# The second tile's first products taken beside the first tile's, with the same weight parts, while the weights are still being converted

## The chip, the cores and the metric

The kernel runs on one core of one Trainium2 chip. Its metric is device time in microseconds; the time of a version is the median of several executions. A profiled execution is recorded separately, with every instruction of the engines: TensorE (PE, its weight loads PEld), VectorE (DVE), ScalarE (ACT), GpSimd (POOL) and SyncE (SP, which issues the DMAs). Every engine takes its instructions in the order in which the program lists them, so an instruction that waits holds up all that stand behind it on its engine.

## The reference

Attention with pooled keys and values, then a gated feed-forward block on its output:

```python
# q, k, v: (8, 8, 576, 64) = batch, heads, sequence, head size; pool = 8, so 72 pooled keys
k_p = k.reshape(B, H, Sp, pool, D).mean(axis=3)
v_p = v.reshape(B, H, Sp, pool, D).mean(axis=3)
scores = scale * np.matmul(q, k_p.transpose(0, 1, 3, 2))
scores = scores - np.max(scores, axis=-1, keepdims=True)
attn = np.exp(scores)
attn = attn / (np.sum(attn, axis=-1, keepdims=True) + 1e-09)
x = np.matmul(attn, v_p)            # then heads are joined: 4608 tokens x 512
a = x @ w_a                         # 512 x 1536
b = x @ w_b                         # 512 x 1536
return (a * b @ w_out)              # 1536 x 512
```

The queries, keys and values are float32; the weights reach the chip as 64-bit floating-point words, which the kernel converts to float32 itself.

## The kernel before

**Precision.** Each float32 operand of a product is split into a high part in the rounded type `fp32r` and a low part, the remainder; a product is then three matmuls (high times high, high times low, low times high). A split is a copy on ScalarE for the high part and a subtraction (`low_part`, L169) on DVE or POOL for the low.

**Tiling.** The 4608 tokens are nine tiles of 512 (`NTILE`). Attention works in 40 chunks of up to 128 tokens that follow the batches (576 tokens each): the first tile has chunks 0 to 3, the second chunks 4 to 8 (of 64, 64, 128, 128 and 128 tokens). A chunk (`chunk`, L343) loads its queries, splits them (`qh`, `ql`), multiplies them with the pooled keys (scores, L379), takes the maximum of each head on DVE (L388, L389), an exponential on ScalarE for each head with its sum (L392), reciprocals (L399, L400) and the normalization (L402, on POOL or DVE), splits the probabilities (`pr`, `rem`), turns them with transposes on TensorE (L447, copied out by ScalarE at L448) and, a block of chunks at a time, multiplies them with the pooled values (L480 to L483). The result is split into `xh` and `xl` (L491 and `low_part`).

**Feed-forward.** For each tile, twelve steps f = 0 to 11 of 128 hidden columns. `ffn_in` (L511) makes 12 matmuls into `psa` and 12 into `psb` (L522 to L524), one PSUM buffer each; ScalarE copies `psa` to `h` (L527, one buffer) and `gated` (L497) multiplies it with `psb` on DVE (L500) and splits the product into `hh` and `hl`. `ffn_out` (L532) of the step before adds 12 matmuls to four accumulators (L543 to L545), which are copied out and stored after the last step (L549 to L552). A step is 36 matmuls; a tile 432.

**Weights.** `convert_weights` (L194) turns the 64-bit words of `w_a`, `w_b` and `w_out` into float32, step by step, with two operations on ScalarE (L210, L211) and three on DVE (L212, L216, L221) for each weight and step; it runs through the first tile, at most two steps ahead. `split_weight` (L228) then makes the parts `jha`/`jla`, `jhb`/`jlb`, `jho`/`jlo`, two buffers each, anew for every tile and step; the low parts of `w_a` and `w_b` are made on DVE in the first tile and on POOL later, those of `w_out` on POOL.

**Order.** The program is listed by hand with a small planner, `Chains` (L71). Each piece of work is a generator that yields after a part of it, with the number of ticks until its next part, or `PE` when it next wants a place on TensorE. `ffn_in` and `ffn_out` call `chains.step()` before every six matmuls: a tick. All pieces due are then listed on their engines, and one that wants TensorE is given its place there. `need` (L507) takes ticks without feed-forward work until something is ready. Ahead of the first product, the program takes ticks until the first tile's attention has been listed (L576). The chunks of the second tile are spread over the steps of the first, 10 ticks apart (`CHUNK_GAP`); those of a later tile are spread over the tile ahead of it. Keys and values of a batch are loaded and pooled by `load_keys` (L238) and `load_values` (L279).

The tag `att` (scores, transposes and value products) has two PSUM buffers, `acc` four. `tmp` is a ring of six buffers for raw queries, conversion intermediates, pooled keys and outputs.

Of the kernel before, what the change touches and what calls it, by code (L numbers as in the profile page):

```python
# [20 lines left out]
P = 128  # L21
# [34 lines left out]

AHEAD = 2
# [4 lines left out]
SPLIT_A, SPLIT_B, SPLIT_O = 1, 4, 4  # L62
PROBS_GAP, VALUE_GAP = 2, 4
CHUNK, CHUNK_LATER, CHUNK_GAP = 34, 32, 10
# [3 lines left out]
EARLY_GAP, VALUES_START, KEYS_START, WEIGHTS_START, CONVERT_AFTER = 1, 2, 4, 10, 5  # L68
# [44 lines left out]
def attn_moe_kernel(ctx: ExitStack, tc: tile.TileContext, q, k, v, vr, wa, wb, wo, out):  # L113
# [3 lines left out]
    ps = ctx.enter_context(tc.tile_pool(name="ps", bufs=1, space=bass.MemoryType.PSUM))  # L117
    chains = Chains()
# [48 lines left out]
    vrems, parts, xtiles, turned, begun = {}, {}, {}, {}, []  # L167
# [26 lines left out]
    def convert_weights(name, j, first):  # L194
# [9 lines left out]
        for f in range(NF):  # L204
# [4 lines left out]
            low, mag = tmp(f"wlow_{name}{f}", I32), tmp(f"wmag_{name}{f}")  # L209
            nc.scalar.activation(mag, hi.bitcast(F32), AF.Abs, scale=SHRINK)  # L210
            nc.scalar.activation(low, lo.bitcast(U32), AF.Copy, scale=2.0**-29)  # L211
            nc.vector.tensor_scalar(  # L212
                out=wi, in0=mag.bitcast(I32), scalar1=0x0FFFFFFF, scalar2=3, op0=ALU.bitwise_and, op1=ALU.logical_shift_left
# [13 lines left out]

    def split_weight(name, x):  # L228
        f = x % NF
        yield from wait(("weight", name, f))  # L230
        hi = sb.tile([P, 512], F32R, tag=f"jh{name}", name=f"jh{name}_{x}")
        lo = sb.tile([P, 512], F32R, tag=f"jl{name}", name=f"jl{name}_{x}")
        nc.scalar.copy(hi, raw[name][:, f, :])  # L233
# [109 lines left out]
    def chunk(i):  # L343
        b, o, n = flat[i]
        t, col = divmod(b * S + o, NT)
        first = i < early
        if first:
            qraw = early_q[:, i]
        else:
            qraw = tmp(f"qraw_{i}").rearrange("p (g s) -> p g s", g=NK)  # L350
            load_raw_queries(i, qraw)
            yield 5
# [6 lines left out]
        yield 1 if first else PROBS_GAP  # L359
# [9 lines left out]
        for g0 in range(0, NK, 2):  # L369
            yield from wait(("keys", b, g0))  # L370
            yield PE
            if first:
                pt = ps.tile([P, 512], F32, tag="acc", name=f"psc_{i}_{g0}", bufs=4)
            else:
                pt = ps.tile([P, 512], F32, tag="att", name=f"psc_{i}_{g0}", bufs=2)
            for j in range(2):
                g = g0 + j
                for x, (qq, w) in enumerate(((qh, 0), (qh, 1), (ql, 0))):
                    nc.tensor.matmul(  # L379
                        pt[:n, j * hk:(j + 1) * hk],  # L380
                        qq[:, g, :n],
                        kd[:, g, w].rearrange("p e s -> p (e s)"),
                        start=(x == 0),
                        stop=(x == 2),
                    )
            hs = slice(2 * g0, 2 * g0 + 4)
            scores = pt[:n, :2 * hk].rearrange("p (h s) -> p h s", h=4)
            nc.vector.tensor_reduce(out=m[:n, hs], in_=scores, axis=AX.X, op=ALU.max)  # L388
            nc.vector.tensor_scalar_mul(m[:n, hs], m[:n, hs], -SCALE)  # L389
            for j in range(4):  # L390
                h = 2 * g0 + j
                nc.scalar.activation(  # L392
                    s[:n, h], scores[:, j], AF.Exp, bias=m[:n, h:h + 1], scale=SCALE, accum_out=z[:n, h:h + 1]
                )
        mark("scores", i)


        yield 1
        nc.vector.tensor_scalar_add(z[:n], z[:n], 1e-9)  # L399
# [18 lines left out]
        yield PROBS_GAP  # L418
# [41 lines left out]
        yield 1 if first else VALUE_GAP  # L460
# [36 lines left out]
    def gated(x, pt, h):  # L497
        hh = sb.tile([P, NT], F32R, tag="hh", name=f"hh_{x}")
        hl = sb.tile([P, NT], F32R, tag="hl", name=f"hl_{x}")
        nc.vector.tensor_tensor(out=h, in0=pt, in1=h, op=ALU.mult)  # L500
        parts["h", x] = hh, hl
        yield 1
# [3 lines left out]

    def need(ready):  # L507
# [148 lines left out]
```

## Time and profile before

| | |
|---|---|
| median of 3 runs | 1119.18 us (1118.94 to 1120.06) |
| the profiled execution, its own time | 1116.74 us |
| its span, from the first to the last instruction | 1115.0 us |
| mean granted TensorE clock | 0.986 |
| TensorE busy, of the span | 1045.9 us (94%) |
| DVE, ACT, POOL busy | 543.8, 594.8, 538.6 us |
| first feed-forward matmul | 59.9 us |
| end of the first tile's output products | 219.3 us |

How to read it: the shares are means over stages that differ. Lines of the timeline give the start, the duration, the engine, the line of the kernel, the operation, output <- input and a count; brackets hold the idle time ahead of it on its engine and what ended it. Matmuls overlap, so the time that one takes from TensorE is the distance between starts, not its duration. A group line gives shapes, count, busy time and mean duration in ns, then the idle time ahead of its instructions. A wait line gives who waited for whom: us in total, times, longest. In a table by stage, each engine's busy time is followed by its number of instructions; PEclk is the granted clock.

### The profile page before, as it was taken

Reading aid. Unit: us, or ns where it says so; the run is one execution under the profiler, and the core shown is the slowest. Engines: PE = TensorE matmul, PEld = TensorE weight load, DVE = VectorE, ACT = ScalarE, POOL = GpSimd, SP = SyncE. Lnnn points to the kernel's source line nnn. Section 1 sums busy time; section 2 is a strip of 40 time slices with the busy share of each in tenths; the row PEclk is TensorE's granted clock in tenths of the full one; section 3 lists DMA queues with packets and bytes.
Section 4 is the critical chain, followed back from the end, with each engine's and each line's share of the span. In section 5 each row is a group of like instructions: output and inputs, shape, how many; then the busy total and the mean of one; then the engine's idle time right before and its main releaser. Section 6 shows DMA issues by size and latency. Waiting matters only on the chain.

```text
span 1115.0 us, 14406 instructions
## 1 busy us (share of the span) xinstructions
PE 1045.9 (94%) x5088; PEld 870.9 (78%) x5088; DVE 543.8 (49%) x839; ACT 594.8 (53%) x1651; POOL 538.6 (48%) x441
## 2 busy tenths in 40 slices
PE   4387888999998999999999999999999999999998
PEld 4276666888887888888887888888887888888887
DVE  7688888632455225632456335643356333332111
ACT  5756766545555455554556455554555455453332
POOL 7102322555555555555556455545546555554442
PEclk9989889999999999999999999999999999999999
DMA  6454443210112001300030003200211020001001
GB/s 209 131 160 123 124 150 126 73 42 1 55 42 85 1 1 41 130 1 1 22 115 14 1 2 102 68 1 1 69 55 48 1 66 1 2 1 38 1 1 38
DMA packets 29879, 59.64 MB, mean 53 GB/s; under 512 B 7120, under 2 KB 7120, under 8 KB 29808
## 3 DMA queue, kind: packets, MB, share of 16 engines
q1 hardware_dynamic: 29808, 58.73, 16.5%
q8 instruction: 40, 0.66, 0.3%
q14 instruction: 31, 0.25, 0.1%
HBM read 49.28 MB, written 9.44 MB: 53 GB/s over the span
## 4 chain that ended last, share of the span: by engine, by line
PE 78%; DVE 13%; ACT 6%; issue 2%; DMA 1%; SPq 0%; DVEq 0%; ACTq 0%
PE psb L522 8%; PE psa L522 8%; PE psa L524 8%; PE psa L523 8%; PE acc L543 8%; PE acc L544 8%; PE acc L545 8%; PE psb L524 8%; PE psb L523 7%; PE psc L379 3%; ACT s L392 3%; DVE vdiag L328 2%; PE ptr L447 2%; DVE vrem L170 1%; DVE h L500 1%
## 5 line engine op out<-in xcount | busy, mean ns | idle before, releaser
L500 DVE TENSOR_TENSOR h<-psb,h 128x512 f32<-128x512 f32 x108 | 74.5, 690 | 310.7 <-PE psb L524 310.6
L170 POOL TENSOR_TENSOR jlb<-wb_raw,jhb 128x512 fp32r<-128x512 f32 x96 | 125.1, 1303 | 201.2 <-ACT jhb L233 201.2
L170 POOL TENSOR_TENSOR jlo<-wo_raw,jho 128x512 fp32r<-128x512 f32 x108 | 152.7, 1414 | 81.0 <-ACT jho L233 51.8
L522 PE MATMUL psb<-xh,jhb 128*128 128x512 f32 x432 | 177.8, 412 | 1.3 <-DVE h L500 1.3
L524 PE MATMUL psb<-xh,jlb 128*128 128x512 f32 x432 | 171.5, 397 | 1.8 <-DVE jlb L170 1.8
L522 PE MATMUL psa<-xh,jha 128*128 128x512 f32 x432 | 172.3, 399 | 0.0
L543 PE MATMUL acc<-jho,hh 128*128 128x512 f32 x432 | 171.5, 397 | 0.0
L527 ACT COPY h<-psa 128x512 f32<-128x512 f32 x108 | 63.5, 588 | 201.9 <-PE psa L524 188.4
L523 PE MATMUL psb<-xl,jhb 128*128 128x512 f32 x432 | 170.8, 395 | 0.0
L524 PE MATMUL psa<-xh,jla 128*128 128x512 f32 x432 | 170.1, 394 | 0.0
L523 PE MATMUL psa<-xl,jha 128*128 128x512 f32 x432 | 169.6, 393 | 0.0
L544 PE MATMUL acc<-jlo,hh 128*128 128x512 f32 x432 | 169.5, 392 | 0.0
L545 PE MATMUL acc<-jho,hl 128*128 128x512 f32 x432 | 169.2, 392 | 0.0
L392 ACT ACTIVATE s<-psc,m 128x72 f32<-128x72 f32 (+1 forms) x320 | 97.9, 318 | 133.1 <-DVE m L389 131.7
L170 POOL TENSOR_TENSOR jla<-wa_raw,jha 128x512 fp32r<-128x512 f32 x96 | 138.4, 1442 | 44.1 <-ACT jha L233 43.7
L402 POOL TENSOR_TENSOR s<-s,z 128x576 f32<-128x576 f32 (+1 forms) x38 | 46.1, 1213 | 223.7 <-PE psb L524 141.0
L170 DVE TENSOR_TENSOR hl<-h,hh 128x512 fp32r<-128x512 f32 x108 | 125.8, 1165 | 38.2 <-ACT hh L503 38.0
L503 ACT CAST hh<-h 128x512 fp32r<-128x512 f32 x108 | 67.1, 622 | 89.4 <-DVE h L500 89.2
L524 PEld LDWEIGHTS psb<-xh,jlb 128*128 128x128 f32 x432 | 82.4, 191 | 20.8 <-DVE jlb L170 2.7
L524 PEld LDWEIGHTS psa<-xh,jla 128*128 128x128 f32 x432 | 81.9, 190 | 17.5
L545 PEld LDWEIGHTS acc<-jho,hl 128*128 128x128 f32 x432 | 81.8, 189 | 17.4
L543 PEld LDWEIGHTS acc<-jho,hh 128*128 128x128 f32 x432 | 81.9, 190 | 16.2
(84 smaller groups left out, 1806.3 us busy)
## 6 DMA issues: line engine op xcount, KB each, us to landing
out<-y SPq DMA_DIRECT2D x36, 256.0 KB, 2.1
kraw<-in_k SPq DMA_DIRECT2D x28, 288.0 KB, 3.4
vraw<-in_v SPq DMA_DIRECT2D x28, 256.0 KB, 3.3
qraw<-in_q SPq DMA_DIRECT2D x28, 256.0 KB, 3.7
words<-in_wa SPq DMA_DIRECT2D x12, 512.0 KB, 3.7
words<-in_wb SPq DMA_DIRECT2D x12, 512.0 KB, 3.6
words<-in_wo SPq DMA_DIRECT2D x12, 512.0 KB, 3.6
vraw<-in_vr SPq DMA_DIRECT2D x14, 192.0 KB, 2.7
```

What stands on the lines that cost most here:

```text
L170: eng.tensor_tensor(out=lo, in0=src, in1=hi.bitcast(F32), op=ALU.subtract)
L392: nc.scalar.activation(s[:n, h], scores[:, j], AF.Exp, bias=m[:n, h:h + 1], scale=SCALE, accum_out=z[:n, h:h + 1])
L402: (nc.vector if first and i % 2 else nc.gpsimd).tensor_tensor(out=s[:n], in0=s[:n], in1=z[:n].unsqueeze(2).broadcast_to([n, H, SP]), op=AL ...
L500: nc.vector.tensor_tensor(out=h, in0=pt, in1=h, op=ALU.mult)
L503: nc.scalar.copy(hh, h)
L522: nc.tensor.matmul(pt, wh[:, c], xh[:, kk], start=(kk == 0), stop=False)
L523: nc.tensor.matmul(pt, wh[:, c], xl[:, kk], start=False, stop=False)
L524: nc.tensor.matmul(pt, wl[:, c], xh[:, kk], start=False, stop=(kk == NK - 1))
L527: nc.scalar.copy(h, pt)
L543: nc.tensor.matmul(acc[c], hh[:, cs], wh, start=(f == 0), stop=False)
L544: nc.tensor.matmul(acc[c], hh[:, cs], wl, start=False, stop=False)
L545: nc.tensor.matmul(acc[c], hl[:, cs], wh, start=False, stop=(f == NF - 1))
```

## The change

The steps of feed-forward work become an explicit list, `order`. In the first tile, from step f = 4 (`LAG`) on, `ffn_in` of the first tile is followed by `ffn_in` of the second for the same f, which uses the same parts of `w_a` and `w_b`; then comes `ffn_out` of the first tile for f - 1. The second tile's gated products of these eight steps are not split at once: they are stored to DRAM (`later`) and fetched back (`fetch_gated`) when the second tile's output products want them. After the first tile, the second does its steps f = 0 to 3 and all of its output products. Tiles from the third on run as before.

For this all chunks of the second tile have to be finished before its step 4; they start from tick 14 of the opening on, 3 ticks apart, with shorter gaps between their parts. The loads of the second batch's keys start 4 ticks later. Starts of weight splits, fetches and chunks are now planned from each item's place in `order`.

Three smaller edits go with it. The softmax subtracts the maximum on DVE, takes one exponential over all heads of a chunk on ScalarE and sums on DVE. From chunk 9 (`SUMMED`) on, the two score matmuls with the same high part of the queries become one of 288 columns, whose halves DVE adds. The magnitude in `convert_weights` is written into the weight's own tile rather than into a temporary.

The places of the parts are counted: `room` lets a split begin only in the order of use and while fewer than two parts of its kind are held, and `drop` gives them back after their last use.

```diff
+SUMMED = 9
+LAG = 4
+IN, OUT = 4, 2
+LEAD_A, LEAD_B, LEAD_O, LEAD_H = 5, 4, 6, 8
 PROBS_GAP, VALUE_GAP = 2, 4
-CHUNK, CHUNK_LATER, CHUNK_GAP = 34, 32, 10
+CHUNK = 32
+SECOND_GAP, SECOND_START = 3, 14
-EARLY_GAP, VALUES_START, KEYS_START, WEIGHTS_START, CONVERT_AFTER = 1, 2, 4, 10, 5
+EARLY_GAP, VALUES_START, KEYS_START, WEIGHTS_START, CONVERT_AFTER = 1, 2, 8, 10, 5
...
-            nc.scalar.activation(mag, hi.bitcast(F32), AF.Abs, scale=SHRINK)
+            nc.scalar.activation(w, hi.bitcast(F32), AF.Abs, scale=SHRINK)
...
+    def room(name, x):
+        while upcoming[name][0] != x or held[name] >= 2:
+            yield 1
+        upcoming[name].pop(0)
+        held[name] += 1
+
+    def drop(*keys):
+        for key in keys:
+            del parts[key]
+            held[key[0]] -= 1
...
+        def less_max(hs, src):
+            nh = hs.stop - hs.start
+            nc.vector.tensor_reduce(out=m[:n, hs], in_=src, axis=AX.X, op=ALU.max)
+            nc.vector.tensor_tensor(
+                out=s[:n, hs], in0=src, in1=m[:n, hs].unsqueeze(2).broadcast_to([n, nh, SP]), op=ALU.subtract
+            )
...
+        else:
+            for g in range(NK):
+                yield from wait(("keys", b, g - g % 2))
+                if g % 2 == 0:
+                    yield PE
+                pt = ps.tile([P, 512], F32, tag="att", name=f"psc_{i}_{g}", bufs=2)
+                nc.tensor.matmul(
+                    pt[:n, :2 * hk], qh[:, g, :n], kd[:, g].rearrange("p w e s -> p (w e s)"), start=True, stop=False
+                )
+                nc.tensor.matmul(
+                    pt[:n, :hk], ql[:, g, :n], kd[:, g, 0].rearrange("p e s -> p (e s)"), start=False, stop=True
+                )
+                nc.vector.tensor_reduce(
+                    out=s[:n, 2 * g:2 * g + 2, :].rearrange("p h s -> p (h s)"),
+                    in_=pt[:n, :2 * hk].rearrange("p (w c) -> p c w", w=2),
+                    axis=AX.X,
+                    op=ALU.add,
+                )
+                if g % 2 and g < NK - 1:
+                    yield 1
+            yield 1
+            less_max(slice(0, H), s[:n])
         mark("scores", i)
         yield 1
+        nc.scalar.activation(s[:n], s[:n], AF.Exp, scale=SCALE)
+        yield 1
+        nc.vector.tensor_reduce(out=z[:n], in_=s[:n], axis=AX.X, op=ALU.add)
...
+    def gated(x, pt, h, kept):
+        nc.vector.tensor_tensor(out=h, in0=pt, in1=h, op=ALU.mult)
+        if kept:
+            later[x] = dram.tile([P, NT], F32, name=f"later_{x}")
+            nc.sync.dma_start(later[x], h)
+            return
+        yield 1
+        yield from split_gated(x, h)
...
+    def fetch_gated(x):
+        h = tmp(f"back_{x}")
+        nc.sync.dma_start(h, later.pop(x))
+        yield LEAD_H - 4
+        yield from split_gated(x, h)
...
+    def ffn_in(t, f):
+        x = t * NF + f
         xh, xl = xtiles[t]
+        kept = t == 1 and f >= LAG
         for name in ("a", "b"):
+            key = name, f if kept else x
+            need(lambda: key in parts)
...
+    order = []
+    for f in range(NF):
+        order.append(("in", 0, f))
+        if f >= LAG:
+            order.append(("in", 1, f))
+        if f:
+            order.append(("out", 0, f - 1, f == 1, False))
+    order.append(("out", 0, NF - 1, False, True))
+    seconds = [*range(LAG, NF)]
+    for f in range(LAG):
+        order.append(("in", 1, f))
+        if f:
+            order.append(("out", 1, f - 1, False, False))
+        order.append(("out", 1, seconds.pop(0), f == 0, False))
+    order.append(("out", 1, LAG - 1, False, False))
+    order += [("out", 1, f, False, f == NF - 1) for f in seconds]
...
+        for i in range(early, sum(t < 2 for t in tile_of)):
+            chains.start(chunk(i), (CHUNKS[0], i), SECOND_START + SECOND_GAP * (i - early))
```

More of the change, by code (lines that the diff above doesn't have):

```diff
@@ L350, in chunk @@
             qraw = tmp(f"qraw_{i}").rearrange("p (g s) -> p g s", g=NK)
+            if soon:
+                yield from wait(("scores", i - 2))
             load_raw_queries(i, qraw)
-            yield 5
+            yield 3 if soon else 5
         yield from wait(("scores", i - 2))
@@ L358, in chunk @@
         low_part(nc.gpsimd if first else nc.vector, ql[:, :, :n], qraw[:, :, :n], qh[:, :, :n])
-        yield 1 if first else PROBS_GAP
+        yield 1 if soon else PROBS_GAP
         yield from wait(("probs", i - 2))
@@ L367, in chunk @@
         hk = 2 * SP
[L369 to L393, printed above, removed]
-                )
@@ L459, in chunk @@
             return
-        yield 1 if first else VALUE_GAP
+        yield 1 if soon else VALUE_GAP
         yield from wait(("values", b))
@@ L527, in ffn_in, with ffn_out @@
                 nc.scalar.copy(h, pt)
-        chains.resume(gated(x, pt, h), PRODUCTS)
+        chains.resume(gated(x, pt, h, kept), PRODUCTS)
     acc = {}
-    def ffn_out(x):
-        t, f = divmod(x, NF)
-        need(lambda: ("o", x) in parts)
-        wh, wl = parts.pop(("o", x))
-        hh, hl = parts.pop(("h", x))
+    def ffn_out(t, f, first, last):
+        x = t * NF + f
+        need(lambda: ("o", x) in parts and ("h", x) in parts)
+        (wh, wl), (hh, hl) = parts["o", x], parts["h", x]
         for c in range(NT // P):
@@ L592, in attn_moe_kernel @@
-        for x in range(NTILE * NF):
-            t = x // NF
-            if t == 0:
-                begun.append(chains.now)
-            need(lambda: have(t))
-            if x + 1 < NTILE * NF:
-                chains.start(split_weight("a", x + 1), SPLITS, SPLIT_A)
-                chains.start(split_weight("b", x + 1), SPLITS, SPLIT_B)
-            chains.start(split_weight("o", x), SPLITS, SPLIT_O)
-            ffn_in(x)
-            if x:
-                ffn_out(x - 1)
-            else:
+        slot = [0]
@@ new lines, in attn_moe_kernel @@
+        for item in order:
+            slot.append(slot[-1] + (IN if item[0] == "in" else OUT))
+        plan = []
+        for n, (kind, t, f, *_) in enumerate(order):
+            x = t * NF + f
+            if kind == "out":
+                plan.append((slot[n] - LEAD_O, split_weight("o", x), SPLITS))
+                if t == 1 and f >= LAG:
+                    plan.append((slot[n] - LEAD_H, fetch_gated(x), SPLITS))
+            elif x and not (t == 1 and f >= LAG):
+                plan.append((slot[n] - LEAD_A, split_weight("a", x), SPLITS))
+                plan.append((slot[n] + IN // 2 - LEAD_B, split_weight("b", x), SPLITS))
@@ new lines, in attn_moe_kernel @@
+        begin_of = {t: slot[order.index(("in", t, 0))] for t in range(2, NTILE)}
+        free = slot[order.index(("in", 0, NF - 1)) + 1]
+        for i in range(len(flat)):
+            b, o, n = flat[i]
+            t = tile_of[i]
+            if t < 2:
+                continue
+            since = free if t == 2 else begin_of[t - 1]
+            share = (b * S + o + n - t * NT) / NT
+            begin_at = since + int((begin_of[t] - since) * share) - CHUNK
+            plan.append((begin_at, chunk(i), (CHUNKS[0], i)))
+            if i + 1 < len(flat) and flat[i + 1][0] > max(b, 1):
+                plan.append((begin_at - KEYS_AHEAD, load_keys(b + 1), KEYS))
+                plan.append((begin_at - KEYS_AHEAD + VALUES_AFTER, load_values(b + 1), KEYS))
@@ L605, in attn_moe_kernel @@
+        plan.sort(key=lambda x: x[0])
+        for n, (kind, t, *where) in enumerate(order):
+            if kind == "in":
+                if t == 0:
+                    begun.append(chains.now)
+                need(lambda: have(t))
+            while plan and plan[0][0] < slot[n + 1]:
+                at, chain, rank = plan.pop(0)
+                chains.start(chain, rank, max(0, at - slot[n]))
+            (ffn_in if kind == "in" else ffn_out)(t, *where)
+            if n == 0:
                 chains.step()
-        chains.step()
```

87 lines of the change are left out of this document (57 added, 30 removed).

## The prediction

> **What bounds the kernel now.** I read the page first (how busy each engine is in 40 slices, and the chain that ended last), then a table of the span cut by stage.
>
> ```profile
> span 1115.0 us, 14406 instructions
> ...
> PE   4387888999998999999999999999999999999998
> ...
> DVE  7688888632455225632456335643356333332111
> ...
> PE 78%; DVE 13%; ACT 6%; issue 2%; DMA 1%; SPq 0%; DVEq 0%; ACTq 0%
> ```
> ```profile
> core 0: us, PE busy (x) PEld busy (x) DVE busy (x) ACT busy (x) POOL busy (x), PEclk, DMA share, GB/s
> 0.00:34.00 34.00, 13.67 (x60) 12.41 (x61) 23.69 (x47) 19.89 (x88) 20.73 (x29) 1.00 0.58 189
> 34.00:59.90 25.90, 11.65 (x63) 10.78 (x63) 18.42 (x33) 15.94 (x34) 3.30 (x4) 1.00 0.51 163
> 59.90:106.20 46.30, 40.10 (x184) 31.39 (x183) 37.17 (x66) 31.14 (x84) 7.49 (x6) 0.93 0.44 134
> 106.20:219.30 113.10, 96.88 (x456) 78.08 (x456) 92.24 (x147) 75.85 (x198) 37.57 (x29) 0.92 0.35 111
> 219.30:1115.00 895.70, 883.59 (x4333) 738.21 (x4332) 372.29 (x548) 452.02 (x1250) 469.54 (x373) 1.00 0.11 34
> ```
>
> The stages are the opening (to the first feed-forward product at 59.9 us), steps f = 0 to 3 of the first tile (to 106.2), its steps 4 to 11 (to 219.3), and the rest. In the rest TensorE is busy 883.59 of 895.70 us: that stage is TensorE's. Before it DVE fills up (80% and 82% busy in the two middle rows), and TensorE idles 6.2 + 16.2 = 22.4 us there, besides running below full clock (0.93 and 0.92).
>
> ```profile
> 247.98 0.39 PE L522 MATMUL psa<-xh,jha 128*128 128x512 f32 x1
> ...
> 250.70 0.39 PE L522 MATMUL psb<-xh,jhb 128*128 128x512 f32 x1
> ```
> ```profile
> 72.59 0.63 PE L522 MATMUL psb<-xh,jhb 128*128 128x512 f32 x1
> 73.02 0.63 PE L523 MATMUL psb<-xl,jhb 128*128 128x512 f32 x1
> ```
>
> These are starts in the timeline. Warm, 12 products of one weight take 250.70 - 247.98 = 2.72 us, so 0.227 us each; after a stall they start 0.43 us apart. The first tile's 432 products and the 24 of the second's first step, done by 219.3, need 456 x 0.227 = 103.5 us, and that stretch lasts 159.4 us. The difference is attention, idling and half speed. The waits of TensorE there:
>
> ```profile
> PE ptr L447 <- ACT p L448: 6.3, 4, 3.2
> PE ptr L447 <- ACT pr L411: 5.2, 3, 2.4
> PE ptr L447 <- DVE xl L170: 4.3, 2, 3.4
> ```
>
> They are the second tile's attention, which stands in TensorE's order between products and isn't ready: 15.8 of the 22.4 us.
>
> **The change, stage by stage.** From f = 4 on, each step of the first tile is followed by the same step of the second with the same parts: 8 x 24 = 192 products come forward. The second tile's five chunks (4 to 8) start at tick 14, three ticks apart, instead of being spread over the first tile, and all must be done before its first product. The softmax changes too.
>
> ```profile
> L392 ACT ACTIVATE s<-psc,m 128x72 f32<-128x72 f32 x256 | 78.5, 321 | 110.6 <-DVE m L389 109.4 <-PE psa L524 1.2
> ...
> L388 DVE TENSOR_REDUCE m<-psc 128x4 f32<-128x288 f32 x64 | 29.2, 456 | 61.8 <-PE psc L379 61.5
> ...
> L253 DVE TENSOR_REDUCE kp<-kraw 128x72 f32<-128x576 f32 x28 | 20.1, 740 | 1.8 <-DMA kraw<-in_k 1.8
> ...
> L389 DVE TENSOR_SCALAR m<-m 128x4 f32<-128x4 f32 x64 | 13.4, 209 | 2.2
> ...
> L170 DVE TENSOR_TENSOR xl<-po,xh 128x384 fp32r<-128x384 f32 x16 | 8.9, 554 | 11.3 <-ACT xh L491 11.2
> ...
> L388 DVE TENSOR_REDUCE m<-psc 64x4 f32<-64x288 f32 x16 | 7.1, 444 | 12.5 <-PE psc L379 12.5
> ```
>
> Softmax, per chunk: two scalings leave (2 x 0.209); two subtractions over 288 scores come, which the trace lacks (bounds: 0.21, the scaling, and 0.554, a subtraction over 384; I take 0.45, by columns nearest the latter and the 0.456 reduction), and one sum over 576, like the key reduction: 0.74. DVE: +0.9 + 0.74 - 0.42 = 1.2 us. ScalarE has one exponential instead of eight of 0.32 us, which relieves it, but the eight mostly waited for DVE (109.4 us).
>
> Opening. DVE is busy 23.69 + 18.42 = 42.1 of 59.9 us. It gains 4 x 1.2 = 4.9, and chunks 4, 5 and half of 6: low parts about 1.9, maxima and subtractions 2 x 1.8 + 1.8, sums and reciprocals 2 x 1.1, together 9.5; 2.6 us of value sums of batch 1 (four of 0.68, the first row below) move behind. That is 54 us. DVE idles 7.5 us from 34 us on, which takes most of it; the remainder would extend the opening by about 4, and ScalarE's relief (its exponentials wait in turn with DVE) takes some back. Bounds 57 and 67; I take **61**.
>
> ```profile
> L305 DVE TENSOR_REDUCE vp<-vraw 128x64 f32<-128x512 f32 x28 | 18.0, 675 | 2.4 <-DMA vraw<-in_v 2.4
> ```
> ```profile
> L170 POOL TENSOR_TENSOR jlo<-wo_raw,jho 128x512 fp32r<-128x512 f32 x108 | 152.7, 1414 | 81.0 <-ACT jho L233 51.8 <-DVE vdiag L328 29.2
> ...
> L170 POOL TENSOR_TENSOR pr<-s,pr 128x512 fp32r<-128x512 f32 x32 | 43.1, 1348 | 6.5 <-ACT pr L411 6.5
> ...
> L402 POOL TENSOR_TENSOR s<-s,z 128x576 f32<-128x576 f32 x30 | 35.4, 1179 | 179.3 <-PE psb L524 141.0 <-DVE z L400 38.3
> ```
>
> Steps 0 to 3. DVE's 37.2 us lose chunks 4 and 5, of 64 rows (four maxima of 0.44 and what follows them, 4.0), and gain the rest of chunk 6 (1.0), all of 7 and 8 (2 x 3.8), five blocks' low parts (2.2) and 2.5 of values: 46.5. POOL gets 5 x 3 us of attention in this stretch too (1.35 + 1.18 and the remainders), and this matters to DVE:
>
> ```profile
> 86.18 1.53 DVE L221 CUSTOM_DVE_ANT_0 wo_raw<-wo_raw,wlow_o 128x1024 uint16<-128x1024 uint16 x1
> ...
> 90.61 0.69 DVE L221 CUSTOM_DVE_ANT_0 wa_raw<-wa_raw,wlow_a 128x1024 uint16<-128x1024 uint16 x1
> ```
> ```profile
> 85.76 1.40 POOL L402 TENSOR_TENSOR s<-s,z 64x576 f32<-64x576 f32 x1 [2.91 <-ACT hh L503]
> ```
>
> The same conversion takes 1.53 us beside that POOL operation and 0.69 alone. By how often they met, I add 4: 50.5. At the 80% of the row before it lasts 63 us, at 90% and without the 4 us 52; I take **58**. (TensorE alone needs 132 x 0.227 = 30 and some 16 for attention.)
> [...]
>
> Steps 4 to 11. TensorE has 8 x 60 = 480 products, 109 us, and about 3 of attention of tile 2. DVE keeps the 92.2 us of the row, less some 20 for chunks 5 to 8, plus 8 x 0.69 for the gated products: about 78, so it isn't the bound. But psb is one buffer: the second tile's psb products start 2.72 us after the first's end, and until then DVE must have read it. Before, the output products stood between.
>
> ```profile
> 101.50 0.39 PE L524 MATMUL psb<-xh,jlb 128*128 128x512 f32 x1
> ```
> ```profile
> 109.67 0.68 DVE L500 TENSOR_TENSOR h<-psb,h 128x512 f32<-128x512 f32 x1
> ...
> 196.23 0.69 DVE L500 TENSOR_TENSOR h<-psb,h 128x512 f32<-128x512 f32 x1 [1.73 <-PE psb L524]
> ```
>
> Under tile 1's attention DVE came 7.8 us late (109.67 after 101.89); at 196.23, that attention nearly over, it waited for TensorE. Eight steps cost between 0 and 8 x 5.1; with the attention gone the second row is nearer, so I take 7 in all: **119**.
>
> ```profile
> out<-y SPq DMA_DIRECT2D x36, 256.0 KB, 2.1
> ...
> words<-in_wa SPq DMA_DIRECT2D x12, 512.0 KB, 3.7
> ```
>
> The gated products that wait go out on SP's queue right behind the product; behind them stand word loads, which are needed a step or more later and land in 3.7 us. h, one buffer, comes free 2.1 us after the store starts (as out<-y lands); its next writer is 5.4 us away. The fetch leads its use by eight ticks, 10.9 us. Their cost is nothing; without that cover it would be a landing, 2 to 4 us, in each of eight steps. Sixteen weight splits are saved on ScalarE and POOL, off the path. The conversion's magnitude now goes straight into the weight tile: the same operations, a buffer less; no cost.
>
> The rest. 132 + 480 = 612 products are then done, against 456 at 219.3: 156 x 0.227 = 35.4 us off the 895.7.
>
> ```profile
> 459.77 0.34 PE L379 MATMUL psc<-kdiag,qh 128*128 128x144 f32 x2
> ...
> 460.40 0.44 PE L522 MATMUL psa<-xh,jha 128*128 128x512 f32 x1
> ```
>
> Six score products of 144 columns take 0.63 us, 0.105 each. From chunk 9 on two of three become one of 288, by columns 288/512 x 0.227 = 0.128: 0.315 becomes 0.233, four times in 25 full chunks: 8.2 us. DVE pays 2.7 us a chunk (four summings like the 0.456 maximum, maximum and subtraction over 576 at 0.74 each and the sum, less 1.33), of which it has plenty (372 of 896 busy). The second tile's output products at its end come five in a row, 2.72 us each, and want a split from POOL each (1.41 us): +2; fewer waits for ScalarE: -2. 895.7 - 35.4 - 8.2 = **852**.
>
> Sum: 61 + 58 + 119 + 852 = 1090 us of span. The profiled execution took 1116.74, 1.74 more than its span, and the median is 1119.18, 4.2 more: **1094 us**.
>
> **The rivals.**
> *DVE's gaps swallow the work.* For it: 7.5 us idle in the second row, and waits that five interleaved chunks could fill. Then the opening takes 59, steps 0 to 3 50 (TensorE's 46 and little else), steps 4 to 11 113, and half of the rest's 12.1 us of idling goes: 846. Span 1068, time 1072.
> *The single psb buffer becomes the wait (slower than before).* If DVE stays as late as at 109.67 in steps 4 to 11, each loses 7.8 - 2.72 = 5.1 us, 41 in all instead of 7: 1128. It decides from 1119.2 - 1094 + 7 = 32 us, 4 a step, a lateness of 6.7 us. For it: the row at 109.67, and DVE's 78 of 119 us leave it behind at times. Against: it was late beside attention, which is over by then.
> [...]
> *The scores drain late.* Four score tiles per chunk now pass through two buffers that DVE empties. At 0.8 us a chunk in 31 chunks 25 us are lost: 1119, no change. Against: in the last row DVE is busy 42%.
>
> **How the numbers follow.** Forecast 0.50, with its own range 1080 to 1108; gaps filled 0.23; psb 0.14; drains 0.13, half of it still a gain. A measurement here tells about 0.2% from no change. Faster 0.79, the same 0.07, slower 0.14. The bounds of the unknown terms and four fifths of the chance give 1066 to 1122.
>
> **What would show it.** Right: the first product at 61 us; the second tile's f = 4 near 119; its last input product near 238; 36 products in 8.2 us afterwards; a full chunk's scores about 0.9 us. Wrong: TensorE waiting for L500's counterpart over 4 us a step; an opening over 67; score tiles that wait for DVE's summing; half-speed products between 120 and 240 us.

## The result and the profile after

| | before | changed |
|---|---|---|
| median (four runs of each) | 1119.06 us | 1088.99 us |
| lowest and highest | 1118.61, 1120.06 | 1088.57, 1089.11 |
| the profiled execution, its own time | 1116.74 us | 1089.11 us |
| its span | 1115.0 us | 1087.3 us |

The ratio is 0.9729, with a 95% interval of 0.9713 to 0.9746: 2.7% less time. The forecast was 1094 us, in a range of 1066 to 1122.

From the page of the changed kernel, the rows that answer to those of before (40 slices of 27.2 us; shares of the chain that ended last):

```profile
span 1087.3 us, 13572 instructions
...
PE   4479999999999999999999999999998999999998
...
DVE  8879967854675347534684346643567344322112
...
PE 84%; DVE 11%; ACT 2%; DMA 1%; issue 1%; SPq 0%; POOL 0%; DVEq 0%; ACTq 0%
```

TensorE is full from the fourth slice on instead of from the eighth; one slice late in the run shows an 8 that was not there before. The table by stage, cut at the same landmarks as the sum (first feed-forward product; second tile's first early step, after 132 products; 612 products done):

```profile
core 0: us, PE busy (x) PEld busy (x) DVE busy (x) ACT busy (x) POOL busy (x), PEclk, DMA share, GB/s
0.00:70.20 70.20, 34.71 (x165) 30.16 (x165) 55.04 (x103) 34.89 (x76) 29.74 (x39) 1.00 0.52 167
70.20:119.40 49.20, 46.25 (x232) 36.01 (x231) 46.10 (x78) 34.74 (x72) 14.56 (x12) 0.97 0.37 116
119.40:237.30 117.90, 116.45 (x540) 96.47 (x539) 84.27 (x141) 58.05 (x108) 18.38 (x15) 1.00 0.38 123
237.30:1087.30 850.00, 837.68 (x4033) 696.99 (x4031) 404.28 (x621) 387.57 (x779) 450.32 (x360) 0.99 0.12 38
```

| term of the sum | forecast (bounds), us | measured, us |
|---|---|---|
| opening | 61 (57 to 67) | 70.2 |
| steps 0 to 3 | 58 (52 to 63) | 49.2 |
| 480 products, steps 4 to 11 of the first tile | 119 | 117.9 |
| the rest | 852 | 850.0 |

The first two together are 119.4 us against 119. What TensorE waits for in the third and fourth stage is short (us in total, times, longest):

```profile
PE psa L595 <- DVE xl L182: 0.7, 1, 0.7
PE psb L594 <- DVE h L551: 0.6, 1, 0.6
PE po L535 <- ACT p L500: 0.2, 1, 0.2
```
```profile
PE psc L431 <- DVE ql L182: 6.4, 2, 3.2
PE ptr L499 <- DVE s L434: 1.1, 1, 1.1
PE psc L428 <- DVE s L434: 0.2, 1, 0.2
```

Two rivals fall with these rows. The wait for the single `psb` buffer is the second line: 0.6 us, not 41. Score tiles that wait for DVE's summing (L434) cost 1.3 us, not 25. But 6.4 us stand in a place where the forecast has none: twice, 3.2 us each, score products wait for the low part of the queries, `ql`, which DVE makes. What DVE does then, in the timeline, beside the same instruction early in the run:

```profile
40.38 0.41 DVE L182 TENSOR_TENSOR ql<-qraw,qh 128x256 fp32r<-128x256 f32 x1
...
567.87 4.77 DVE L182 TENSOR_TENSOR ql<-qraw,qh 128x256 fp32r<-128x256 f32 x1
```

A subtraction of 0.41 us lasts 4.77. Beside it POOL and TensorE:

```profile
567.54 1.15 POOL L454 TENSOR_TENSOR s<-s,z 64x576 f32<-64x576 f32 x1 [4.76 <-ACT jho L258]
568.65 1.28 POOL L182 TENSOR_TENSOR jlb<-wb_raw,jhb 128x512 fp32r<-128x512 f32 x1
569.88 1.26 POOL L182 TENSOR_TENSOR jlo<-wo_raw,jho 128x512 fp32r<-128x512 f32 x1
571.10 1.25 POOL L182 TENSOR_TENSOR pr<-s,pr 64x512 fp32r<-64x512 f32 x1
572.32 0.50 POOL L182 TENSOR_TENSOR rem<-s,rem 64x64 fp32r<-64x64 f32 x1
```
```profile
569.20 0.29 PE L428 MATMUL psc<-kdiag,qh 128*64 128x288 f32 x1
572.70 0.28 PE L431 MATMUL psc<-kdiag,ql 128*64 128x144 f32 x1 [3.20 <-DVE ql L182]
...
573.65 0.63 PE L595 MATMUL psa<-xl,jha 128*128 128x512 f32 x1
574.08 0.63 PE L596 MATMUL psa<-xh,jla 128*128 128x512 f32 x1
```

POOL has operations in a row without a gap from 567.54 on. DVE's subtraction begins 0.33 us into the first and ends at 572.64, 0.29 us after the fourth has ended at 572.35. It ends there although POOL goes on: the fifth operation, `rem`, takes 0.50 us (0.33 in the kernel before, at 339.71). Why it ends behind the fourth and not earlier isn't shown. TensorE stands for 3.20 us, and the products behind the wait start 0.43 us apart instead of 0.227 for some 3 us more; from 572.60 to 576.40 the granted clock reads 0.55. The same happens at 824.91, where the half speed lasts longer (0.51 from 829.70 to 835.80). In the profile before, no `ql` that DVE makes takes longer than 1.72 us.

Below, such a meeting with POOL's operations is called a collision, and DVE's long operation blocked or held: the traces show when each ran and how long it took, not what holds DVE.

Three questions were open. How much of the 30 us does the new order bring, and how much the edits that go with it? What do the two blocked subtractions cost? And could the second tile start its early products at another place for more?

### The profile page after: what moved, and what is told of

Read it like the earlier page. It is cut to its first block, busy times and chain, and to the rows that moved or that the text cites. A ratio compares the mean times of both kernels' runs of the same rounds, so it can differ in the third digit from the quotient of the medians.

```text
span 1087.3 us, 13572 instructions
## 1 busy us (share of the span) xinstructions
PE 1035.1 (95%) x4964; PEld 859.6 (79%) x4964; DVE 589.7 (54%) x941; ACT 515.3 (47%) x1035; POOL 513.0 (47%) x425
## 4 chain that ended last, share of the span: by engine, by line
PE 84%; DVE 11%; ACT 2%; DMA 1%; issue 1%; SPq 0%; POOL 0%; DVEq 0%; ACTq 0%
PE psa L594 9%; PE psb L594 9%; PE acc L616 9%; PE psa L595 8%; PE psa L596 8%; PE acc L618 8%; PE acc L617 8%; PE psb L596 8%; PE psb L595 8%; PE ptr L499 2%; PE psc L428 2%; DVE ql L182 1%; DVE s L399 1%; PE psc L431 1%; PE po L534 1%
## 5 line engine op out<-in xcount | busy, mean ns | idle before, releaser
L182 POOL TENSOR_TENSOR jlb<-wb_raw,jhb 128x512 fp32r<-128x512 f32 x88 | 114.5, 1301 | 264.1 <-ACT jhb L258 264.1
L182 POOL TENSOR_TENSOR jlo<-wo_raw,jho 128x512 fp32r<-128x512 f32 x108 | 144.0, 1334 | 116.5 <-ACT jho L258 116.5
L594 PE MATMUL psb<-xh,jhb 128*128 128x512 f32 x432 | 171.7, 398 | 0.6 <-DVE h L551 0.6
L596 PE MATMUL psb<-xh,jlb 128*128 128x512 f32 x432 | 168.6, 390 | 0.0
L182 POOL TENSOR_TENSOR jla<-wa_raw,jha 128x512 fp32r<-128x512 f32 x88 | 126.6, 1438 | 68.0 <-ACT jha L258 64.0
L564 ACT CAST hh<-h 128x512 fp32r<-128x512 f32 x100 | 62.2, 622 | 91.4 <-DVE h L551 86.7
L182 DVE TENSOR_TENSOR hl<-h,hh 128x512 fp32r<-128x512 f32 x100 | 90.2, 902 | 24.2 <-ACT hh L564 23.9
L595 PEld LDWEIGHTS psa<-xl,jha 128*128 128x128 f32 x432 | 82.8, 192 | 15.6 <-DVE xl L182 1.1
L594 PEld LDWEIGHTS psa<-xh,jha 128*128 128x128 f32 x432 | 82.6, 191 | 15.0
L594 PEld LDWEIGHTS psb<-xh,jhb 128*128 128x128 f32 x432 | 81.2, 188 | 16.1 <-DVE h L551 1.0
```

Source lines behind the costliest of these rows:

```text
L182: eng.tensor_tensor(out=lo, in0=src, in1=hi.bitcast(F32), op=ALU.subtract)
L564: nc.scalar.copy(hh, h)
L594: nc.tensor.matmul(pt, wh[:, c], xh[:, kk], start=(kk == 0), stop=False)
L595: nc.tensor.matmul(pt, wh[:, c], xl[:, kk], start=False, stop=False)
L596: nc.tensor.matmul(pt, wl[:, c], xh[:, kk], start=False, stop=(kk == NK - 1))
```

## The experiments

Each is compared with the kernel before, run on the same chip beside it. Before's median was 1118.5 to 1119.7 us in all of them; ratios have their 95% interval.

**The order undone.** All small edits, the attention of the second tile ahead of the first product and the planner stay; the second tile's steps come after the first's.

```diff
-        kept = t == 1 and f >= LAG
+        kept = False
...
-        if f >= LAG:
-            order.append(("in", 1, f))
...
-    for t in range(2, NTILE):
+    for t in range(NTILE):
```

> The changed kernel with the second tile's twelve steps back behind the first tile's, no gated product through DRAM; the early start of the second tile's attention and the small edits stay. Mine: without the interleaved products steps 4 to 11 are paced by DVE: its 84.3 us there less 5.5 of gated products, 79, at 94% busy 84 us, against 118 - 192 x 0.227 = 74.4 for the same work now, so 10 us slower than the changed kernel, 1099. Rival 'the early attention did it': with the attention gone the steps run at TensorE's 8.2 to 9 us each, 1089 to 1092. Rival 'the interleaving is all': these eight steps take the 113 us that they took before, 39 more, 1128.

Measured: 1098.42 us, 0.9816 (0.9801 to 0.983): 9.4 above the changed kernel. The stages show what the early products do: without them the stretch up to the first tile's last output products took 86.5 us for 324 products, 0.267 each, against 117.9 us for 480, 0.246 each. The rest shows that the 9.4 is not the order's alone, as this line from its waits says:

```profile
PE psc L431 <- DVE ql L182: 9.1, 3, 3.2
```

The blocked subtraction strikes three times here instead of twice. The total came where it was expected; part of its reason was another.

**Three products again.** `SUMMED` is set so high that no chunk takes the wide score product.

```diff
-SUMMED = 9
+SUMMED = 99
```

> The changed kernel with three score products of 144 columns for all chunks, not only for the first nine. Mine: 25 full chunks at 0.33 us more, 8 us slower, 1097. Rival 'the drains give it back': the two buffers that DVE has to empty cost what the wider product saves, 1089 within 2. DVE loses 31 summings of four either way.

Measured: 1092.35 us, 0.9762 (0.9745 to 0.9778): 3.4 above the changed kernel, neither theory's number. With three products the order within a chunk changes, and of TensorE's waits for `ql` one of 2.8 us is left:

```profile
PE psc L414 <- DVE ql L182: 2.8, 1, 2.8
```

DVE's subtraction is blocked even so, and three times: for 4.79 us at 320.60 and 5.03 at 577.32 and 832.66. Twice TensorE doesn't need it yet. So what a blocked operation cost here depended on who waited for it. Over the whole run TensorE idles 3.6 us less than in the changed kernel; so 3.4 net is what is left of the term of 8.2 us. By itself the product is worth more, as a later pair shows.

**The old softmax for the first nine chunks.** Exponentials by head on ScalarE, with their sums, wherever the scores aren't summed on DVE.

```diff
-                less_max(slice(2 * g0, 2 * g0 + 4), pt[:n, :2 * hk].rearrange("p (h s) -> p h s", h=4))
+                hs = slice(2 * g0, 2 * g0 + 4)
...
+                nc.vector.tensor_scalar_mul(m[:n, hs], m[:n, hs], -SCALE)
+                for j in range(4):
+                    h = 2 * g0 + j
+                    nc.scalar.activation(
+                        s[:n, h], scores[:, j], AF.Exp, bias=m[:n, h:h + 1], scale=SCALE, accum_out=z[:n, h:h + 1]
+                    )
```

> The changed kernel with the softmax of before (scaled maximum, eight exponentials with their sums on ScalarE) for chunks 0 to 8; later chunks stay. Mine, that DVE's work sets the time to the second tile's first product at 127 us: 9 x 1.2 = 11 us of DVE less there, of which 8 come through, 1081. Rival 'the exponentials sit in the chain': 9 x 1.7 us more of ScalarE, part of it ahead of transposes, 1094 to 1100.

Measured: 1094.85 us, 0.9784 (0.9769 to 0.9798): 5.9 slower than the changed kernel, where DVE's relief should have made it faster. The first product comes at 74.8 us instead of 70.2, though DVE is busy only 48.9 us ahead of it, against 55.0. In the opening two waits of TensorE now end at the exponentials (`s`, L427), 6.6 us in all:

```profile
PE psc L414 <- ACT s L427: 3.7, 1, 3.7
PE ptr L509 <- ACT s L427: 2.9, 1, 2.9
```

ScalarE had itself stood idle ahead of both rows of exponentials, for 2.90 and 2.29 us, until DVE had made the maxima (`m`, L424). Each row of four with its sums then takes 1.3 us. So the longer opening is measured, and less work of DVE does not shorten it; that the exponentials alone make it longer isn't shown.

**The small edits alone.** Before's order, with the new softmax, the wide score product from chunk 9 on and the magnitude in place.

```diff
+SUMMED = 9
...
-            nc.scalar.activation(mag, hi.bitcast(F32), AF.Abs, scale=SHRINK)
+            nc.scalar.activation(w, hi.bitcast(F32), AF.Abs, scale=SHRINK)
...
+        nc.scalar.activation(s[:n], s[:n], AF.Exp, scale=SCALE)
+        yield 1
+        nc.vector.tensor_reduce(out=z[:n], in_=s[:n], axis=AX.X, op=ALU.add)
```

> The kernel before with the small edits alone: the new softmax, one wide score product from chunk 9 on, the magnitude in place; order and starts as before. Mine: 8 us less from the score products, the softmax about even, 1109 to 1112. Rival 'ScalarE's relief is the gain': the waits of the first tile for ScalarE's copies, 11.5 us and the half speed behind them, go too, 1092 to 1100. Rival 'DVE pays': the first tile's steps, 82% busy on DVE, get 6 us longer, 1115 to 1119.

Measured: 1088.46 us, 0.9726 (0.9712 to 0.9741): as fast as the whole change, and less than any of the three theories allowed. This is the result that matters most. Its table by stage (opening, first tile, rest):

```profile
0.00:58.20 58.20, 25.55 (x120) 23.16 (x121) 48.39 (x83) 28.54 (x61) 22.99 (x33) 1.00 0.57 184
58.20:211.40 153.20, 133.83 (x634) 107.64 (x633) 137.15 (x220) 95.61 (x191) 45.24 (x35) 0.93 0.40 123
211.40:1086.00 874.60, 870.76 (x4213) 725.71 (x4211) 395.11 (x638) 399.09 (x800) 462.97 (x374) 1.00 0.11 34
```

The rest falls from 895.70 to 874.60 us: 21.1. Idling goes from 12.1 to 3.8 (8.3 us), and TensorE's busy time falls by 12.8. With three score products (a run below) the rest takes 884.2 us, so 9.6 are the wide product; what is left of the 12.8, 3.2 us, comes near what half speed took in the rest of before: the granted clock reads 0.67 from 345.17 to 350.00 and 0.69 from 858.72 to 863.00, behind two of the waits below, which loses 4.83 x 0.33 + 4.28 x 0.31 = 2.9 us. Before, the rest's one large wait was for ScalarE's copies of the transposed probabilities, and here that row is gone:

```profile
PE ptr L447 <- ACT p L448: 7.7, 5, 3.5
```

At first sight that is ScalarE, relieved of eight short exponentials a chunk. The timeline of before says otherwise. Around the longest of the five waits, ScalarE, DVE and TensorE:

```profile
339.55 0.41 ACT L356 CAST qh<-qraw 128x256 fp32r<-128x256 f32 x1
344.13 0.62 ACT L503 CAST hh<-h 128x512 fp32r<-128x512 f32 x1 [4.18 <-DVE h L500]
344.66 0.64 ACT L448 CAST p<-ptr 128x256 fp32r<-128x256 f32 x2
```
```profile
335.97 6.81 DVE L328 SCALAR_TENSOR_TENSOR vdiag<-vp,vdiag 64x256 fp32r<-64x256 f32 x2
342.70 0.68 DVE L170 TENSOR_TENSOR vrem<-vwide,vrem 32x512 fp32r<-32x512 f32 x1
343.41 0.69 DVE L500 TENSOR_TENSOR h<-psb,h 128x512 f32<-128x512 f32 x1
```
```profile
345.17 0.36 PE L447 MATMUL ptr<-ident,rem 64*96 64x64 f32 x2 [3.52 <-ACT p L448]
```

ScalarE stands idle for 4.18 us. Its copy `p` is behind `hh`, `hh` needs DVE's gated product `h`, and `h` is behind two operations into `vdiag` (the pooled values' low part) that take 6.81 us. With the small edits the same pair takes 0.86 to 1.90 us behind the opening. While the 6.81 us last, POOL runs six operations from 335.57 to 342.49 with no gap over 0.1 us. (The first of the pair ends at 338.60, behind POOL's one small gap of 0.09 us; the second is held for 4.15.) So the kernel before has the same collision as the changed one, at another operation of DVE, and the name at the end of its wait line is that of an engine that was waiting too. The next two waits in length, 1.54 us at 600.97 and 1.55 at 858.72, look the same: the pair takes 4.32 and 4.33 us there, and ScalarE stands idle for 3.27 us both times. This was tried by itself:

**Before, with the values two ticks earlier.** The softmax and the amount of ScalarE's work stay; its copies of the pooled values move along.

```diff
-KEYS_AHEAD, VALUES_AFTER = 18, 16
+KEYS_AHEAD, VALUES_AFTER = 18, 14
```

> The kernel before, with its softmax and its order as they are; only the pooled values of a later batch are made two ticks earlier (2.8 us), so that DVE's two operations into vdiag, which the profile of before shows at 4.3 to 6.8 us a pair beside a run of POOL operations (335.97, 593.16, 850.90; 0.86 us where POOL leaves them alone), fall into POOL's idle time ahead of that run. [...] Theory that the long exponentials are what makes the copies late: nothing changes in ScalarE's work, so the waits stay at 6 to 8 us and the time at 1118 to 1120. If the blocked place only moves to another DVE operation (ql or hl), vdiag is short, one of these takes over 3 us and the time stays above 1114.

Measured: 1113.34 us (1112.15 to 1115.92), 0.9956 (0.9942 to 0.9971): 5.6 us less. With `vdiag` out of POOL's way the author had expected 1107 to 1113, waits for `p` below 2 us and a rest of 884 to 890; the time is 0.3 above that range and well below the 1118 to 1120 of the other theory. The waits for `p` fall from 7.7 to 5.1 us, not below 2, and the rest misses its range too. The collision is only partly avoided: `vdiag` costs DVE 18.5 us instead of 27.2 over the run, but `vrem`, right behind it, is now blocked:

```profile
591.75 3.28 DVE L170 TENSOR_TENSOR vrem<-vwide,vrem 32x512 fp32r<-32x512 f32 x1
```

The same at 849.11, for 3.31 us. The rest took 892.5 us, 3.2 less than before; 1.4 came earlier. A shift that touches no exponential shortens these waits. With ScalarE idle ahead of the three longest, its load is not what made these; the run alone leaves open how much of the 7.7 us is the collision's. What in the small edits moved POOL's run away from `vdiag` altogether was not separated.

**The order alone.** The changed kernel with the old softmax and three products in every chunk; the magnitude in place stays.

```diff
-SUMMED = 9
+SUMMED = 99
...
-                less_max(slice(2 * g0, 2 * g0 + 4), pt[:n, :2 * hk].rearrange("p (h s) -> p h s", h=4))
+                hs = slice(2 * g0, 2 * g0 + 4)
```

> The changed kernel's order and starts with the softmax and the three score products of before for all chunks (the magnitude in place stays). Theory 'the small edits are the gain and the order gives nothing lasting' (from before_softmax at 1088 against the changed kernel's 1089): 1112 to 1119. Theory 'both gain, but overlap': the order alone is worth the 17 us of my sum (35.4 of products come forward, less 18 by which the second tile's last early product lies later), 1100 to 1105.

Measured: 1100.97 us, 0.984 (0.9825 to 0.9856): 17.6 us less than before by itself, inside the range of "both gain, but overlap". The edits alone gain 31, and both together 30.

**The small edits without the wide product.** As the small edits alone, with `SUMMED = 99`.

```diff
-SUMMED = 9
+SUMMED = 99
```

> The kernel before with the new softmax for all chunks but three score products throughout. Theory 'ScalarE's relief': most of the 31 us of before_softmax is that ScalarE no longer stands ahead of its copies of the transposes; the wide product is only its 8: 1095 to 1098. Rival 'the score products are the gain': 1110 or more.

Measured: 1099.23 us, 0.9829 (0.9813 to 0.9845), 1.2 above the range of the theory that it is nearest to; but as the timeline of before shows, it was not ScalarE's load that made the long waits. So the softmax and the magnitude in place bring 19 us of the 31, the vanished collision among them, and the wide product, where nothing is blocked, 10.8.

**Later chunks' low parts earlier.** The gap between the loading and the scores of a later chunk is four ticks longer, and these chunks start four ticks earlier, so the scores stay where they were.

```diff
-CHUNK = 32
+CHUNK = 36
...
-        yield 1 if soon else PROBS_GAP
+        yield 1 if soon else PROBS_GAP + 4
```

> The changed kernel with the chunks of the third tile and later begun 4 ticks earlier and those 4 ticks put between the queries' low part and the scores. [...]

Measured: 1084.53 us (1084.44 to 1087.75; the profiled execution is the longest), 0.9695 (0.9679 to 0.9711). The author had expected 1078 to 1081 if the two waits of 3.2 us go, with some 5 us of half speed behind them, and 1087 to 1091 if another wait takes their place; the time lies between. `ql` is out of the way, but another of DVE's operations meets the same run of POOL's, beginning at 572.89 here:

```profile
574.47 3.84 DVE L182 TENSOR_TENSOR hl<-h,hh 128x512 fp32r<-128x512 f32 x1 [0.69 <-ACT hh L564]
```

`PE psc L428 <- DVE s L434` rises to 6.7 us in five waits: the summing stands behind the blocked operation. The collision has moved to the next subtraction in DVE's queue. Not every operation is held: `h` in the kernel before takes its usual 0.69 us at 599.21 while POOL makes `jlo`.

**One tick.** All later chunks start one tick (six products, 1.4 us) later. Nothing else changes.

```diff
-CHUNK = 32
+CHUNK = 31
```

> The changed kernel with the chunks of the third tile and later begun one tick later (31 for 32 ticks ahead). Counted from a tile's start the old order began them at 72 x share - 31, the new one at 72 x share - 32; the weight splits start at the same ticks in both. Theory 'one tick makes the collision': the old order with the new softmax takes 769.5 us from its 864th product to the end without a wait of TensorE, the changed kernel 784.0; with the tick given back the changed kernel takes about 770, 14 us less in all: 1074 to 1077. Rival 'the new way of starting splits makes it': 1085 to 1090.

Measured: 1078.13 us (1077.59 to 1079.68), 0.9631 (0.9615 to 0.9646): 1.0% below the changed kernel, and the fastest of all, though 1.1 above the range of its theory. Cut at the landmarks (70.3, 120.2 and 238.8 us), 612 products are done 1.5 us later than in the changed kernel; the gain stands in the rest alone:

```profile
238.80:1076.40 837.60, 832.47 (x4033) 693.67 (x4031) 387.99 (x622) 387.43 (x779) 446.80 (x360) 1.00 0.12 38
```

837.6 against 850.0 us: 7.2 of the 12.4 are idling (12.3 to 5.1), 5.2 less busy time, of which the changed kernel's two stretches at clocks of 0.55 and 0.51 make 3.80 x 0.45 + 6.10 x 0.49 = 4.7. The same chunk's subtraction, and POOL beside it:

```profile
570.15 0.20 DVE L452 RECIPROCAL z<-z 64x8 f32<-64x8 f32 x1
570.27 0.39 DVE L182 TENSOR_TENSOR ql<-qraw,qh 128x256 fp32r<-128x256 f32 x1
```
```profile
568.80 1.29 POOL L182 TENSOR_TENSOR jlo<-wo_raw,jho 128x512 fp32r<-128x512 f32 x1
570.42 1.24 POOL L454 TENSOR_TENSOR s<-s,z 64x576 f32<-64x576 f32 x1 [0.33 <-DVE z L452]
```

POOL's normalization now comes behind the weight splits instead of ahead of them and waits 0.33 us for DVE's reciprocal. With that gap the reciprocal and `ql` pass, and `ql` takes 0.39 us. Their neighbours are held, but for one operation of POOL's each: `z` at 568.92 takes 1.20 us beside `jlo`, `hl` at 570.57 takes 1.64 beside `s`. The longer collision comes once here, at 321.01, where `hl` takes 3.90 us; TensorE has no wait over 0.7 us in the rest. Over all chunks, `ql` costs DVE 28.5 us instead of 51.0:

```profile
L182 DVE TENSOR_TENSOR ql<-qraw,qh 128x512 fp32r<-128x512 f32 x28 | 22.9, 819 | 7.3 <-ACT qh L383 7.2
L182 DVE TENSOR_TENSOR ql<-qraw,qh 128x256 fp32r<-128x256 f32 x8 | 5.6, 706 | 2.2 <-ACT qh L383 2.2
```
```profile
L182 DVE TENSOR_TENSOR ql<-qraw,qh 128x512 fp32r<-128x512 f32 x28 | 36.7, 1310 | 2.3 <-ACT qh L383 2.2
L182 DVE TENSOR_TENSOR ql<-qraw,qh 128x256 fp32r<-128x256 f32 x8 | 14.3, 1788 | 3.8 <-ACT qh L383 3.8
```

The first pair is this version, the second the changed kernel.

**One tick the other way.**

```diff
-CHUNK = 32
+CHUNK = 33
```

> The changed kernel with those chunks begun one tick earlier still (33). Theory 'one tick makes the collision': another place of POOL's burst beside the weight splits, so another time; from the theory alone I can't say which way, 1076 to 1095. Rival 'the tick doesn't matter': 1088 to 1090.

Measured: 1084.38 us, 0.9681 (0.9664 to 0.9698). One `ql` is blocked, for 5.03 us at 321.9. The time depends on the tick, not on a trend: 1078, 1089 and 1084 us for 31, 32 and 33.

**The order undone, at the better tick.**

```diff
-CHUNK = 32
+CHUNK = 31
...
-        kept = t == 1 and f >= LAG
+        kept = False
```

> No interleaved products and no trip through DRAM, as in no_interleave, with the later chunks' start one tick later, as in chunk31: what the interleaving itself buys once the collision is out of the way. From the stages: without it steps 4 to 11 and what follows took 86.4 us for 324 products, with it 117.9 for 480; 156 x 0.227 = 35.4 of products for 31.5 us, so it buys 4: chunk31's 1078 plus 4, 1080 to 1084. Rival 'the interleaving buys what no_interleave lost, 9': 1087 or more.

Measured: 1083.54 us, 0.9685 (0.9668 to 0.9702). This is inside the range that was expected. With no blocked `ql` on either side, taking the second tile's products beside the first's is worth 1083.5 - 1078.1 = 5.4 us. The second tile's early attention and the new planning stay on both sides; against the small edits alone (1088.5 us), all that is new at the better tick is worth 10.3.

**Early products from the seventh step on, second tile's attention later.**

```diff
-LAG = 4
+LAG = 6
...
-CHUNK = 32
-SECOND_GAP, SECOND_START = 3, 14
+CHUNK = 31
+SECOND_GAP, SECOND_START = 3, 20
...
-    order.append(("out", 1, LAG - 1, False, False))
+    order.append(("out", 1, LAG - 1, False, not seconds))
```

> chunk31 with the second tile's attention begun six ticks later (20) and its products beside the first tile's from f = 6 instead of 4 on. Theory 'DVE's work only moves': the opening gets shorter by what the steps before the second tile's first product get longer, the total within 4 of chunk31, 1074 to 1082. Rival 'the opening is where the early attention costs': the opening falls from 70 to 62 and most of that stays, 1069 to 1073.

Measured: 1089.21 us (1087.12 to 1090.86), 0.9729 (0.971 to 0.9747). Both theories missed. The first product does come earlier, at 64.1 us, but the stretch behind it then holds the attention that was moved:

```profile
64.10:155.50 91.40, 79.52 (x371) 64.34 (x370) 75.60 (x130) 57.33 (x116) 25.24 (x21) 0.88 0.39 120
...
251.20:1089.10 837.90, 832.82 (x4033) 693.82 (x4031) 385.63 (x619) 384.80 (x773) 446.48 (x360) 1.00 0.11 34
```

TensorE idles 11.9 us from 64.1 to 155.5, 9.1 of it for ScalarE's copies (`p`, L500) ahead of transposes and scores, and its granted clock reads 0.88 there. Its 612 products are done at 251.2 us, those of the version with tick 31 at 238.8; from there both take as long, 837.9 and 837.6 us. So all that is lost is lost by then. Here unfinished attention cost TensorE more between products than ahead of them; two numbers were changed at once, so this is one case and no rule.

## Why the prediction was right, and where it was not

**The total was right**, 1089 against 1094, inside the forecast's own range of 1080 to 1108. Not all of its terms were: the first two lie outside their bounds, one of the prediction's own signs of being wrong was there (an opening over 67), and the fourth holds two errors that cancel. That the sum comes so near is in part luck.

**Opening 61, measured 70.2: the step that failed is "DVE idles 7.5 us from 34 us on, which takes most of it".** The work was right: 54 us of DVE were forecast, 55.0 came. But the idle time did not take it in. DVE idled 17.8 of 59.9 us before and 15.2 of 70.2 now, so 13 us of added work displaced 2.6 us of idling. The runs tell which part of the work it was. With the small edits alone DVE has 48.4 us of work, 6.3 more than before, and the opening is shorter, 58.2 us: the new softmax does go into DVE's idle time. What else comes into the opening, the second tile's attention above all, adds 6.7 us more of DVE and 12.0 us of time. The starts on TensorE at the end of the opening, first with the small edits alone, then in the changed kernel:

```profile
58.02 0.41 PE L510 MATMUL po<-p,vrem 96*128 96x256 f32 x1
58.23 0.59 PE L549 MATMUL psa<-xh,jha 128*128 128x512 f32 x1
```
```profile
64.73 0.70 PE L414 MATMUL psc<-kdiag,qh 128*128 128x144 f32 x2 [2.14 <-DVE xl L182]
...
70.19 0.79 PE L594 MATMUL psa<-xh,jha 128*128 128x512 f32 x1
```

In the one the first feed-forward product starts right behind the last value product of the first tile. In the other this last value product starts at 62.17, and then scores and transposes of the second tile stand in TensorE's order, with waits of 2.14 and 1.20 us for DVE, until 70.19. So 7.8 of the 12.0 us come behind the first tile's last value product and 4.2 ahead of it. The prediction priced the early chunks by DVE's time alone and put their place in TensorE's order, ahead of the first product, at nothing. What makes the 4.2 us was not taken apart.

**Steps 0 to 3 58, measured 49.2, below the bound of 52: mis-sized twice.** DVE's work was 46.1 us; the prediction had 50.5, of which 4 were meetings with POOL that did not show in the sum. And DVE was 94% busy instead of 87%; TensorE waited 2.9 us. The two stages hold 101.1 us of DVE's work together, against 104.5 forecast. That 119.4 equals 119 to a fraction is luck: one stage was 9 us too short in the sum, the other 9 too long.

**Steps 4 to 11, 119 and 117.9: right,** with the reason given for it. DVE had 84.3 us of work (78 forecast) and was late for `psb` once, by 0.6 us, with the attention over. The trip of the gated products through DRAM shows in no wait of TensorE; it was not taken out by itself.

**The rest, 852 and 850.0: the value was right and its composition wrong in two terms.** The first is "fewer waits for ScalarE: -2", for which the prediction shows no row. On the old order the edits took 21.1 us from the rest, 9.6 by the wide product and 11.5 by idling (8.3) and half speed (about 3) that went away. By the name in the wait line these waits are ScalarE's. Followed one step further back, the three longest (6.6 of 7.7 us) are DVE's, blocked beside POOL.
The second is a wait that was not in the sum: the new place of the same collision, `ql`. One tick's shift took 12.4 us from the rest. So some 10 us less were missing on one side and 12 more on the other; that they cancel is luck. DVE's meetings with POOL were weighed in steps 0 to 3, where they cost nothing that can be seen; they decided in the later tiles, in both kernels, where DVE is less than half busy.

**"But the eight mostly waited for DVE" was true and no reason to count little on ScalarE's relief.** Ahead of both long waits in the opening the old exponentials waited for DVE, as said. Even so the old softmax in nine chunks cost 5.9 us, 4.6 of them in the opening. An engine's idle time does not prove that its work is out of the way.

**"DVE's gaps swallow the work" came true in part**: steps 0 to 3 took 49.2 (that rival's 50), the opening did not take 59.

**The change itself** brings less through its order than it seems. Counted in the trace, two tiles' worth of products (864) are done at 325.2 us before, 316.5 with the order alone, 315.4 with the edits alone, 303.3 with both. There the gains add up and more (-8.7, -9.8, -21.9). From there to the end it takes 789.8, 783.2, 770.6 and 784.0: the changed kernel is 13.4 us behind the edits alone, and one tick gives 12.3 of that back (771.7).

**Open:** which of the early waits make the two parts gain more together than apart; why the tick of 32 lines up POOL's run and DVE's subtraction only in some chunks; and whether the old kernel with all its collisions gone would keep more of the distance.

## What to carry to other kernels

Split a change with several edits into its parts before crediting the main one: here the small edits alone gave 0.9726, as much as the whole, and the second tile's early products were worth 5.4 us once no `ql` was blocked. Look for an instruction many times as long as its twin, on half-idle engines too and behind the engine that a wait line names, and try the neighbouring ticks before judging a design: 31, 32 and 33 gave 1078, 1089 and 1084 us. Idle time on an engine takes in added work only where nothing else in the new work's chain holds up what follows: here the softmax's 6.3 us went into DVE's gaps, and the second tile's attention, which also stands ahead of the first product on TensorE, did not.

## What the runs showed of the hardware

One DVE subtraction was held through four POOL operations that followed each other without a gap (0.41 us became 4.77, and up to 5.03 in other runs); two operations into `vdiag` in the kernel before took 6.81 us beside six (0.86 at 452.62 with the small edits). In the version with tick 31, where POOL had a gap of 0.33 us, the subtraction took 0.39. After a wait of 3.20 us the following products started 0.43 us apart for about 3 us. The mean granted clock of that stage, 0.99, doesn't show this; over the 3.8 us behind the wait it reads 0.55. What a wait line names can be an engine that was itself waiting: ScalarE stood idle for 4.18 us ahead of the copy for which TensorE waited 3.52.
